# Inducing-point attention and a gated layer on one core: the last four 512-token outputs evacuated in two halves, and a new written-out order

## The chip, the cores and the metric

The kernel runs on one core of a Trainium2 chip. The metric is the device time of one execution in microseconds (us); three runs of the kernel before gave 278.44, 278.89 and 279.71 us. A core has five engines that each work through their own queue in order: TensorE (PE, with PEld for its weight loads), VectorE (DVE), ScalarE (ACT), GpSimd (POOL) and SyncE (SP), which here issues nearly all transfers. Engines wait for each other by semaphores. TensorE writes into PSUM, eight banks of 512 fp32 values in each of 128 partitions; ACT and DVE read PSUM, POOL does not.

## The reference, cut to what matters

Input `x` is 4 batches of 12800 tokens with 128 channels. `inducing` has 32 rows.

```python
def mab(q, kv):
    s = scale * (q @ kv.transpose(0, 2, 1))
    s = s - s.max(-1, keepdims=True)
    a = np.exp(s)
    a /= a.sum(-1, keepdims=True) + 1e-09
    return a @ kv
h = mab(I, x)                      # 32 rows per batch, over 12800 tokens
x = mab(x, h)                      # 12800 rows per batch, over 32 rows
...
for k in range(K):                 # K = 5, causal
    gate_pre += conv_w[k][None, None, :] * xp[:, k:k + S, :]
gate = 1.0 / (1.0 + np.exp(-gate_pre))
val = x @ w_val
return (gate * val @ w_out)
```

## The kernel before, in words

Each batch's tokens are cut into four strips of 3200, which sit side by side in the 128 partitions as four groups of 32. A strip is cut into seven chunks of mostly 416 to 512 tokens (`SIZES`). For each batch the work is:

- `load_xt`, `load_xk` (SP): the tokens with channels in the partitions (`xt`), and with tokens in the partitions (`xk`). In batch 0 `xk` is made on chip: `make_xk` transposes on PE (L315) and copies out of PSUM on ACT (L112) or DVE (L114).
- `s1` (PE L335, evacuated by DVE L351 with a running maximum), `gmax` (DVE L363, then L387 and four L373 on POOL or DVE), `e1` (exponential on ACT L395, 32x32 transposes on DVE L400), `h` (PE L419, summed by DVE L436 to L440): the first attention. `h` of the last chunks needs the maxima of all chunks.
- `prep`, `prep2`, `prep3`, `prep_out`: the 32 rows `hT` are normalised (PE L454, DVE L460 to L462), folded into the weights of the second part (POOL L487, L488, L493; PE L527; copies L112/L114), and scales are made (`osc`: four L555 and L556 on POOL or DVE).
- `s2` (PE L590, DVE L601), `joint` (DVE maximum L613, POOL L619, ACT L625, DVE sum L631 to L636, POOL L642, DVE L647, then ACT L653 and POOL L661 write the attention weights as two fp16 parts into the long strips `P1`, `P2`): the second attention's weights.
- `visit` (PE L676 for the gate's five taps, L685 for the values; ACT L747 tanh; DVE L756 gate times value), `halves` (ACT L768 and POOL L773 split the product into two fp16 parts `gh`, `gl`; `gl` has two buffers), `outp` (PE L782; evacuation with the scale `osc` by DVE L815 or ACT L817 into a tile; store by SP L822). One output is one chunk of one strip, up to 512 tokens by 128 channels, in one PSUM bank.

Nothing is scheduled at build time. Every piece of work is an entry of `Plan.ops`; `launch` emits the entries in the order of the table `TURN`, and each engine's queue has its share of them in that order. `MOVED` lists entries that go to their alternative engine (an evacuation from ACT to DVE, the small `f1` of `gmax` and `prep_out` from POOL to DVE), `BANK` gives each PSUM tile its bank, `FULL` lists outputs that PE makes with 128-column weights instead of four groups of 32. The tables were found by a search outside the kernel. Semaphore waits follow from the tiles that an instruction reads and writes.

The last two chunks of the last batch are the end of the program: chunk 5 has 512 tokens, and its four outputs use the large tiles `ss` and `et` in place of `os`; chunk 6 has 160, and its outputs come two strips at a time and skip the fp16 split.

Of the kernel before, what the change touches and what calls it, by code (L numbers as in the profile page):

```python
# [15 lines left out]
ALU = mybir.AluOpType  # L16
# [10 lines left out]
SP = 1024.0  # L27
# [57 lines left out]
def tile_kernel(ctx: ExitStack, tc: tile.TileContext, xt, xk, indT_in, w64, out):  # L85
# [13 lines left out]
    st = {}  # L99
# [27 lines left out]
    def two(key):  # L127

        return st[key].rearrange("p (a b) -> p a b", a=2)
# [658 lines left out]
    def outp(k, rs):  # L788
# [19 lines left out]

        def ev(j=len(plan.ops)):
            o = sb(pw, os, [P, OSW if os[0] == "os" else 1024])[:, :m * n]  # L810
            a = st[key][:, :n]
            if m == 2:
                o, a = o.rearrange("p (a b) -> p a b", a=2), two(key)[:, :, :n]
            if on(j) is V:
                V.tensor_scalar(o, a, st["osc", b], None, ALU.mult)  # L815
            else:
                S.activation(o, a, AF.Copy, scale=st["osc", b])  # L817

        j = op("ACT", ev, [i], [os], [key, ("osc", b)], size=m * n, alt="DVE")
# [5 lines left out]
        op("SP", store, [j], [], [os], size=m * n * 512)  # L825
# [175 lines left out]
```

## Time and profile before

| | |
|---|---|
| median of 3 runs | 278.89 us (278.44 to 279.71) |
| profiled execution | 278.53 us, of which the span of the trace is 276.4 us |
| PE busy | 263.7 us (95% of the span) |
| DVE busy | 227.6 us (82%) |
| ACT busy | 196.2 us (71%) |
| POOL busy | 194.4 us (70%) |
| moved by DMA | 73.48 MB, 266 GB/s over the span |
| PE's granted clock | 1.00 in nearly every stretch: its level of 2.4 GHz |

The busy times overlap. PE's busy time is the largest; the rest of the span is PE's waits, its start and what follows its last matmul. The stages are plain in the trace: batch 0 is loaded and summed until 32 us, its weights are made until 45 us, then the visits run with the next batch's attention beside them until about 230 us, and the last visits and outputs run alone. After the last matmul there is one evacuation, one store and its landing.

### The profile page before, as it was taken

The page shows a single profiled execution, that of the slowest core. Times are in us where ns is not written, and L with a number is a line of the kernel's source. Part 1 is how long each engine was busy: PE and PEld are TensorE (multiplying, and loading weights), DVE is VectorE, ACT ScalarE, POOL GpSimd, SP SyncE. Part 2 cuts the span into 40 slices and gives each one's busy share as a digit, 9 for nine tenths or more (in the row PEclk, how much of TensorE's full clock was granted, in tenths as well). Part 3 has the DMA queues.
Part 4 walks back from the last instruction along what each step waited for, and adds up shares of the span by engine and source line. Part 5 has one row for each costly group of instructions (what it writes and reads, how often), then busy time and mean ns, then how long its engine had stood idle before and what let it go on. Part 6 is the DMA issues. An engine that isn't in the chain of part 4 may idle for free.

```text
span 276.4 us, 10872 instructions
## 1 busy us (share of the span) xinstructions
PE 263.7 (95%) x4655; PEld 142.3 (51%) x4655; DVE 227.6 (82%) x441; ACT 196.2 (71%) x257; POOL 194.4 (70%) x152
## 2 busy tenths in 40 slices
PE   8989987999999999999999999999999999999993
PEld 4567634766434473475454356656353445443551
DVE  0688899989999977979999799869979997785680
ACT  2547248696588897875877877858878697887764
POOL 1011068976768895985799739876998898997691
PEclk9999999999999999999999999999999999999999
DMA  7999699799989889659989997633134143344467
GB/s 223 408 408 385 224 409 407 262 364 407 348 275 384 314 284 411 263 198 359 365 272 398 329 384 231 256 129 143 58 114 161 64 169 121 115 162 168 154 231 274
DMA packets 30255, 73.48 MB, mean 266 GB/s; under 512 B 3456, under 2 KB 12800, under 8 KB 30208
## 3 DMA queue, kind: packets, MB, share of 16 engines
q1 hardware_dynamic: 30064, 72.79, 71.9%
q8 instruction: 36, 0.59, 0.9%
q14 instruction: 11, 0.09, 0.1%
q10 hardware_dynamic: 144, 0.02, 0.0%
HBM read 46.57 MB, written 26.21 MB: 263 GB/s over the span
## 4 chain that ended last, share of the span: by engine, by line
PE 57%; DVE 16%; DMA 12%; ACT 4%; issue 4%; POOL 3%; SPq 1%; DVEq 0%; ACTq 0%; POOLq 0%
PE banks L676 20%; PE banks L782 17%; PE banks L419 6%; PE banks L590 5%; DMA xt<-in_xt_dram 4%; PE banks L685 4%; DVE tg L756 4%; PE banks L335 3%; DMA raw<-in_w_dram 3%; DMA xk<-in_xk_dram 2%; DMA out_dram<-os 2%; PE banks L315 2%; DVE e L601 2%; ACT os L817 2%; DVE os L815 2%
## 5 line engine op out<-in xcount | busy, mean ns | idle before, releaser
L773 POOL TENSOR_TENSOR gl<-tg,gh 128x1024 f16<-128x1024 f32 (+4 forms) x54 | 106.2, 1972 | 26.3 <-PE banks L782 12.5
L676 PE MATMUL banks<-P,W 32*128 32x512 f16 (+5 forms) x1680 | 105.5, 352 | 1.3 <-ACT W L112 1.0
L676 PEld LDWEIGHTS <-W 32*128 32x128 f16 x1680 | 54.3, 92 | 38.2 <-issue 8.6
L747 ACT ACTIVATE tg<-banks,gsc 128x1024 f32<-128x1024 f32 (+5 forms) x56 | 55.3, 1018 | 22.6 <-PE banks L676 21.4
L756 DVE SCALAR_TENSOR_TENSOR tg<-tg,banks 128x1024 f32<-128x1024 f32 (+5 forms) x56 | 60.5, 1096 | 5.7 <-PE banks L685 4.9
L782 PE MATMUL banks<-gh,wo 128*32 128x448 f16 (+6 forms) x642 | 61.6, 359 | 0.8 <-DVE tg L756 0.6
L768 ACT CAST gh<-tg 128x1024 f16<-128x1024 f32 (+4 forms) x54 | 52.0, 969 | 10.3 <-DVE tg L756 9.3
L782 PEld LDWEIGHTS <-wo 128*32 128x32 f16 (+1 forms) x963 | 31.8, 97 | 38.5 <-issue 14.8
L685 PE MATMUL banks<-P,W 32*128 32x512 f16 (+5 forms) x336 | 41.7, 353 | 2.3 <-ACT tg L747 1.5
L815 DVE TENSOR_SCALAR os<-banks,osc 128x448 f32<-128x448 f32 (+4 forms) x49 | 32.4, 688 | 11.0 <-PE banks L782 9.5
L782 PE MATMUL banks<-gl,wo 128*32 128x448 f16 (+7 forms) x321 | 40.2, 358 | 0.0
L817 ACT ACTIVATE os<-banks,osc 128x512 f32<-128x512 f32 (+4 forms) x57 | 34.9, 646 | 7.5 <-PE banks L782 6.1
L642 POOL TENSOR_TENSOR e<-e,z 128x1024 f32<-128x1024 f32 (+7 forms) x17 | 25.0, 1468 | 7.1 <-ACT tg L747 2.2
L661 POOL TENSOR_TENSOR P<-pt,P 128x1024 f16<-128x1024 f32 (+7 forms) x17 | 27.9, 1640 | 1.8 <-ACT P L653 1.7
L619 POOL TENSOR_TENSOR e<-e,m 128x1024 f32<-128x1024 f32 (+7 forms) x17 | 24.9, 1470 | 5.4 <-DVE m L613 4.8
L419 PE MATMUL banks<-xk,et 128*32 128x129 f32 x800 | 26.0, 274 | 0.3 <-DVE et L400 0.3
L419 PEld LDWEIGHTS banks<-xk,et 128*32 128x32 f32 x800 | 23.1, 110 | 5.9 <-issue 3.0
L335 PE MATMUL banks<-xt,indT 128*32 128x512 f32 (+5 forms) x224 | 25.1, 557 | 0.0
L590 PE MATMUL banks<-xt,hT 128*32 128x512 f32 (+5 forms) x224 | 24.4, 553 | 0.6 <-ACT tg L747 0.5
L351 DVE TENSOR_SCALAR_CACHE_REDUCE ss<-banks 128x1024 f32<-128x1024 f32 (+8 forms) x17 | 15.9, 933 | 8.6 <-PE banks L335 8.4
L685 PEld LDWEIGHTS <-W 32*128 32x128 f16 x336 | 14.2, 92 | 14.1 <-issue 11.6
L395 ACT ACTIVATE ss<-ss,ng 128x1024 f32<-128x1024 f32 (+8 forms) x17 | 15.5, 922 | 7.0 <-DVE ng L373 6.7
(98 smaller groups left out, 254.4 us busy)
## 6 DMA issues: line engine op xcount, KB each, us to landing
xt<-in_xt_dram SPq DMA_DIRECT2D x28, 512.0 KB, 8.1
xk<-in_xk_dram SPq DMA_DIRECT2D x25, 451.5 KB, 6.8
xt<-in_xt_dram SPq DMA_DIRECT2D x23, 448.0 KB, 7.6
out_dram<-os SPq DMA_DIRECT2D x36, 256.0 KB, 2.9
out_dram<-os SPq DMA_DIRECT2D x40, 224.0 KB, 2.6
xk<-in_xk_dram SPq DMA_DIRECT2D x15, 516.0 KB, 7.0
out_dram<-os SPq DMA_DIRECT2D x20, 240.0 KB, 2.7
out_dram<-os SPq DMA_DIRECT2D x4, 208.0 KB, 4.9
```

What stands on the lines that cost most here:

```text
L335: T.matmul(s[32 * r:32 * r + 32, at:at + n], c_["indT"], st[xkey][:, o:o + n // 32, r, :], start=True, stop=True)
L419: T.matmul(t[32 * s:32 * s + 32, :P + 1], st[et][:, at + 32 * i:at + 32 * i + 32], st[xs[c][0]][:, xs[c][1] + i, :], start=j < R, stop=j > ...
L590: T.matmul(s[32 * r:32 * r + 32, at:at + n], st["hT", b], st[xkey][:, m:m + n // 32, r, :], start=True, stop=True)
L676: T.matmul(two(("ps", "g", b, c, r // 2))[:, r % 2, :n], st["W", b][q, w, k, :], st[("P1", "P2")[e]][q, o:o + n], start=u == 0, stop=u == ...
L685: T.matmul(two(("ps", "v", b, c, r // 2))[:, r % 2, :n], st["W", b][q, w, TAPS, :], st[("P1", "P2")[e]][q, o:o + n], start=u == 0, stop=u ...
L747: S.activation(t[:, :, :n], two(("ps", "g", b, c, p))[:, :, :n], AF.Tanh, scale=st["gsc", b])
L756: V.scalar_tensor_tensor(t, t, 1.0, two(("ps", "v", b, c, p))[:, :, :n], ALU.add, ALU.mult)
L768: S.copy(sb(pw, g1, [P, 2, 512], F16)[:, :, :n], st[tg][:, :, :n])
L773: on(j).tensor_tensor(sb(pw, g2, [P, 2, 512], F16)[:, :, :n], st[tg][:, :, :n], st[g1][:, :, :n], ALU.subtract)
L782: T.matmul(t[q], w[:, q], x, start=j == 0, stop=j == len(terms) - 1)
L815: V.tensor_scalar(o, a, st["osc", b], None, ALU.mult)
L817: S.activation(o, a, AF.Copy, scale=st["osc", b])
```

## The change

`outp` gains a second evacuation for the four outputs of the last full chunk (those in `ss` and `et`): ACT takes columns 0 to 255, DVE columns 256 to 511, and the store waits for both. With the four new entries all entry numbers from there on shift, and the tables are new throughout.

```diff
+        cut = n // 2 if os[0] != "os" and m == 1 else m * n
+
         def ev(j=len(plan.ops)):
             o = sb(pw, os, [P, OSW if os[0] == "os" else 1024])[:, :m * n]
             a = st[key][:, :n]
             if m == 2:
                 o, a = o.rearrange("p (a b) -> p a b", a=2), two(key)[:, :, :n]
+            else:
+                o, a = o[:, :cut], a[:, :cut]
...
-        j = op("ACT", ev, [i], [os], [key, ("osc", b)], size=m * n, alt="DVE")
+        def ev2():
+            V.tensor_scalar(st[os][:, cut:n], st[key][:, cut:n], st["osc", b], None, ALU.mult)
+
+        js = [op("ACT", ev, [i], [os], [key, ("osc", b)], size=cut, alt="DVE" if cut == m * n else None)]
+        if cut < m * n:
+            js.append(op("DVE", ev2, [i], [], [os, key, ("osc", b)], size=n - cut))
...
-        op("SP", store, [j], [], [os], size=m * n * 512)
+        op("SP", store, js, [], [os], size=m * n * 512)
...
 TURN = [
-    0, 1, 3, 17, 18, 19, 20, 21, 22, 25, 23, 24, 4, 27, 26, 2, 28, 33, 38, 29, 31, 63, 34, 65, 64, 66, 73, 35, 32,
+    0, 1, 19, 21, 17, 18, 20, 22, 25, 4, 23, 24, 27, 26, 3, 28, 33, 38, 48, 2, 34, 39, 29, 63, 31, 40, 35, 64, 32,
```

What the tables move is seen on the engines' queues. In the changed kernel the evacuations stand at L819 (DVE), L821 (ACT) and L824 (DVE, second halves), the store at L831; lines above 800 are shifted, lower ones are not.

The start of SP's queue: the pieces of batch 0's `xt` and the weights `raw`. Before:

```order
L263 DMA xt<-in_xt_dram 128x640
L263 DMA xt<-in_xt_dram 128x384
L263 DMA xt<-in_xt_dram 128x896
L263 DMA xt<-in_xt_dram 128x768
L263 DMA xt<-in_xt_dram 128x1024 x6
L187 DMA raw<-in_w_dram 128x261
```

Changed:

```order
L263 DMA xt<-in_xt_dram 128x896
L263 DMA xt<-in_xt_dram 128x1024
L263 DMA xt<-in_xt_dram 128x640
L263 DMA xt<-in_xt_dram 128x384
L263 DMA xt<-in_xt_dram 128x768
L263 DMA xt<-in_xt_dram 128x1024 x3
L187 DMA raw<-in_w_dram 128x261
```

The first pieces of chunks 1 and 2 come ahead of chunk 0, and `raw` moves ahead of two pieces of 512 KB, those of chunk 3. The four pieces behind it are the same.

DVE's queue where batch 0's weights are made, from the maximum of the second `s2` piece (L613, 13 columns) on. Before:

```order
L613 TENSOR_REDUCE m_535<-e 128x13
L631 TENSOR_REDUCE z<-e 128x8
L633 TENSOR_SCALAR z<-z 128x24
L634 RECIPROCAL z<-z 128x8
L636 MEMSET z 32x1
L351 TENSOR_SCALAR ss,mx<-banks 128x960
L647 STREAM_TRANSPOSE pt<-e 128x256
L631 TENSOR_REDUCE z<-e 128x13
```

Changed:

```order
L613 TENSOR_REDUCE m_546<-e 128x13
L351 TENSOR_SCALAR ss,mx<-banks 128x448
L508 TENSOR_SCALAR w_548<-banks,vs 128x32
L509 SCALAR_TENSOR_TENSOR w_548<-banks,vs,w_548 128x32
L631 TENSOR_REDUCE z<-e 128x8
L633 TENSOR_SCALAR z<-z 128x24
L634 RECIPROCAL z<-z 128x8
L636 MEMSET z 32x1
L631 TENSOR_REDUCE z<-e 128x13
L633 TENSOR_SCALAR z<-z 128x39
L634 RECIPROCAL z<-z 128x13
L647 STREAM_TRANSPOSE pt<-e 128x256
```

The next batch's evacuation of 448 columns (L351) moved from ahead of the first L601 to behind the second maximum, and the sum of the second piece now stands ahead of the first piece's L647; the evacuation of 960 columns moved behind it.

The end of DVE's queue, with the semaphores that each instruction waits for. Changed:

```order
L819 TENSOR_SCALAR os<-banks,osc 128x320 [waits DMAHW5_49,PE_49]
L824 TENSOR_SCALAR et<-banks,osc 128x256 [waits Activation_49]
L824 TENSOR_SCALAR ss<-banks,osc 128x256 [waits Activation_49]
L819 TENSOR_SCALAR os<-banks,osc 128x320 [waits DMAHW6_49,DVE_49,PE_49]
L824 TENSOR_SCALAR et<-banks,osc 128x256 [waits Activation_49]
L824 TENSOR_SCALAR ss<-banks,osc 128x256 [waits Activation_49]
```

The four new second halves each wait for one semaphore, ACT's, and the four first halves on ACT (L821) for PE's. Before, the four outputs were whole evacuations on ACT:

```order
L817 ACTIVATE et<-banks,osc 128x512 [waits DVE_49,PE_49]
L817 ACTIVATE ss<-banks,osc 128x512 [waits PE_49]
L817 ACTIVATE et<-banks,osc 128x512 [waits PE_49]
L817 ACTIVATE ss<-banks,osc 128x512 [waits DVE_49,PE_49]
```

## Rows read from the trace of the kernel before

**Rows 1.** The page: busy us of each engine, share of the span, instructions.
```profile
PE 263.7 (95%) x4655; PEld 142.3 (51%) x4655; DVE 227.6 (82%) x441; ACT 196.2 (71%) x257; POOL 194.4 (70%) x152
```

**Rows 2.** Busy time by stretch: from:to, length, busy us (PE, PEld, DVE, ACT, POOL), clock, DMA share, GB/s.
```profile
0.00:10.00 10.00, 8.74 (x47) 4.61 (x48) 1.97 (x9) 2.78 (x4) 1.32 (x12) 1.00 0.82 276
10.00:20.00 10.00, 8.73 (x102) 5.70 (x101) 7.67 (x25) 4.76 (x8) 0.52 (x2) 1.00 1.03 414
...
22.10:32.22 10.12, 9.72 (x202) 7.28 (x201) 8.50 (x21) 6.13 (x8) 0.12 (x1) 1.00 0.73 265
32.22:40.72 8.50, 7.40 (x136) 2.76 (x137) 8.00 (x33) 3.10 (x6) 3.96 (x8) 1.00 1.02 409
...
47.35:100.00 52.65, 52.40 (x1041) 29.58 (x1039) 49.19 (x97) 39.66 (x52) 41.30 (x29) 1.00 0.93 329
...
200.00:220.00 20.00, 20.00 (x344) 9.36 (x340) 17.50 (x26) 15.29 (x22) 18.68 (x12) 1.00 0.35 124
```

**Rows 3.** The timeline of the head: start, length, engine, instruction, [idle before and what ended it].
```profile
15.85 1.92 PE L335 MATMUL banks<-xt,indT 128*32 128x512 f32 x16
16.35 0.30 DVE L199 TENSOR_SCALAR bt<-raw 128x261 int32<-128x261 int32 x1 [0.67 <-DMA raw<-in_w_dram]
...
22.10 1.92 PE L335 MATMUL banks<-xt,indT 128*32 128x512 f32 x16
...
32.22 0.33 PE L454 MATMUL banks<-pick,H 128*32 128x32 f32 x16 [0.40 <-DVE H L440]
```

**Rows 4.** The timeline where batch 0's weights are made.
```profile
34.01 0.60 DVE L351 TENSOR_SCALAR_CACHE_REDUCE ss<-banks 128x448 f32<-128x448 f32 x1
...
38.02 1.15 DVE L351 TENSOR_SCALAR_CACHE_REDUCE ss<-banks 128x960 f32<-128x960 f32 x1
...
39.46 0.55 DVE L631 TENSOR_REDUCE z<-e 128x13 f32<-128x416 f32 x1
...
41.59 0.61 DVE L647 STREAM_TRANSPOSE pt<-e 128x416 f32<-128x416 f32 x1
...
43.47 0.97 POOL L661 TENSOR_TENSOR P<-pt,P 128x416 f16<-128x416 f32 x1
...
44.49 0.35 PE L676 MATMUL banks<-P,W 32*128 32x416 f16 x2 [0.24 <-POOL P L661]
```

**Rows 5.** The timeline at two waits of PE for a PSUM bank.
```profile
144.89 0.99 ACT L747 ACTIVATE tg<-banks,gsc 128x896 f32<-128x896 f32 x1
...
145.94 1.33 PE L590 MATMUL banks<-xt,hT 128*32 128x448 f32 x12 [0.46 <-ACT tg L747]
...
227.34 0.87 DVE L601 STREAM_TRANSPOSE e<-banks 128x672 f32<-128x672 f32 x1
...
228.27 0.38 PE L685 MATMUL banks<-P,W 32*128 32x480 f16 x2 [0.42 <-DVE e L601]
```

**Rows 6.** The timeline of the last output.
```profile
271.50 0.40 PE L782 MATMUL banks<-gl,wo 128*32 128x512 f16 x4
...
271.94 0.69 ACT L817 ACTIVATE ss<-banks,osc 128x512 f32<-128x512 f32 x1
...
272.65 0.33 SPq L822 DMA_DIRECT2D out_dram<-ss  x1
```

**Rows 7.** Evacuations by shape: count, busy us, mean ns of one, idle before.
```profile
L817 ACT ACTIVATE os<-banks,osc 128x512 f32<-128x512 f32 x21 | 13.9, 686 | 2.6 <-PE banks L782 2.5
...
L815 DVE TENSOR_SCALAR os<-banks,osc 128x512 f32<-128x512 f32 x15 | 11.0, 745 | 5.1 <-PE banks L782 5.1
...
L815 DVE TENSOR_SCALAR os<-banks,osc 128x416 f32<-128x416 f32 x4 | 2.3, 633 | 0.0
...
L817 ACT ACTIVATE os<-banks,osc 128x224 f32<-128x224 f32 x4 | 1.5, 447 | 1.0 <-PE banks L782 1.0
```

**Rows 8.** The small `f1` instructions: ns of one, minimum, median and maximum, by engine.
```profile
L555 DVE TENSOR_SCALAR u<-qm x12: 201/204/207, 98.3 to 221.8; 32x1 f32<-32x1 f32 x12
L555 POOL TENSOR_SCALAR u<-qm x4: 278/282/286, 45.9 to 47.0; 32x1 f32<-32x1 f32 x4
```

More of the change, by code (lines that the diff above doesn't have):

```diff
@@ L883 @@
 TURN = [
[51 rows of a table removed]
[52 rows of a table added]
 ]
 MOVED = [
[4 rows of a table removed]
[4 rows of a table added]
 ]
 BANK = [
[9 rows of a table removed]
[9 rows of a table added]
 ]
 FULL = [
-    832, 835, 838, 850, 856, 859, 994, 997, 1000, 1003, 1006, 1009, 1012, 1015, 1030, 1033, 1036, 1039, 1042, 1045,
-    1048, 1051, 1054, 1057, 1060, 1063, 1066, 1069, 1072, 1075, 1078, 1081, 1084, 1087, 1093, 1096, 1099,
+    850, 856, 859, 985, 988, 991, 994, 997, 1000, 1003, 1018, 1021, 1024, 1027, 1042, 1045, 1048, 1051, 1054, 1057,
+    1060, 1063, 1066, 1069, 1072, 1075, 1078, 1081, 1084, 1087, 1090, 1093, 1096, 1099, 1102, 1106, 1110, 1114,
+    1118, 1121,
 ]
```

127 rows, old and new, of tables (BANK, MOVED, TURN) are left out of this document.

## The prediction

> **What bounds the kernel now.** I read the page's busy times first, then the windows by stage, then the timelines at the start, where batch 0's weights are made, at PE's waits, and at the end. The busy times [rows 1] say that PE is the engine to watch: 263.7 of 276.4 us. The clock column of the windows stands at 1.00 throughout, the 2.4 GHz level [rows 2], so no term below is a clock. The windows say where PE is not the limit. From 47.35 to 100 us it is busy 52.40 of 52.65 us, but from 32.22 to 40.72 us only 7.40 of 8.50, with DVE at 8.00 [rows 2]. So there are three places where time can be had: the head up to 32.22 us, set by transfers and by a chain through DVE; the making of batch 0's weights after it; and the end, where one evacuation and one store follow PE's last matmul. In between only waits of PE for a PSUM bank or for a late operand count, and they are short: the two that I looked up are 0.46 and 0.42 us [rows 5].
>
> PE's work itself does not change. Both kernels have the same visits, sums and outputs; three more outputs use 128-column weights, which stream the same columns, and I cost that at nothing.
>
> **The halves.** This is the part that the title names, and the order decides it. Each second half on DVE waits for ACT, not for PE: the four L824 rows each name ACT's semaphore. Since the first half is the last thing ACT has done by then, DVE starts when ACT ends, so the halves run one after the other. The last output now: PE's last matmuls begin at 271.50 and run 0.40, ACT starts at 271.94, takes 0.69, and the store issues at 272.65 [rows 6]. An ACT evacuation takes 447 ns at 224 columns and 686 at 512, so 256 take about 447 + 32 x 239/288 = 474 ns. DVE takes 633 at 416 and 745 at 512; along that line 256 take about 633 - 160 x 112/96 = 446 ns, but the lone fixed cost may be more, so I take 0.48 [rows 7]. From ACT to PE a hand-over is 145.88 to 145.94, and from DVE to PE 228.21 to 228.27: 0.06 us [rows 5]. The sum is 0.47 + 0.06 + 0.48 = 1.01 us in place of 0.69: **+0.3 us** at the very end, where nothing covers it. Bounds: 0.2 us for the hand-over makes it +0.5; halves that did overlap would give 0.48 - 0.69 = -0.2. The first three of the four outputs cost nothing: ACT kept up with PE at 0.69 us for a whole one, and either half is shorter. SP's four stores wait for DVE now instead of ACT, with nothing behind them but each other.
>
> The Trainium skill, "PSUM — Partial Sum Buffer", section "PSUM bank collisions raise a hardware error", says that two engines may not be in the same bank and 32-partition group at once, reads against reads included, and that the compiler's scheduler adds a dependency between them. One 512-token output is one bank, so by that rule the two halves cannot run at once, which speaks against the change; the wait in the order has that shape, and no run yet shows its length.
>
> **The head.** `raw` (0.27 MB) now goes ahead of chunk 3's pieces (1.05 MB). Counting bytes down SP's queue (128 partitions by the columns of its rows, 4 bytes each, 8 for `raw`), `raw` ended at 4.79 MB before. The first 10 us move 2.76 MB and the next run at 0.414 MB/us [rows 2], so 4.79 MB have moved at 14.9 us; DVE got `raw` at 16.35 [rows 3], about 1.45 us later. The same count gives chunk 3 at 4.52 MB: 14.25 + 1.45 = 15.7, and its `s1` began at 15.85 [rows 3], so this stage runs as its data arrive. Now chunk 3 ends at 4.79 MB and its `s1` begins about 0.5 us later. The last piece of batch 0 ends at 6.89 MB in both orders: 20.0 + 1.45 = 21.45 us. The `s1` on it began at 22.10 before [rows 3], behind three groups of transposes. In the new order PE has the same three groups before it, but reaches them sooner, since `h` of chunks 0 and 1 and chunk 4's transposes are done back to back rather than in the gaps. So it can begin at 21.5: -0.6 us, and no earlier. From there both orders have the same list on PE: one `h`, three groups of eight transposes, four `h`; it took 10.12 us with 9.72 busy [rows 2], the last 0.40 a wait for DVE's sum [rows 3]. DVE's chain behind that `s1` is the same, with one weights instruction less in it; I take 0.3 of the 0.40. The head: **-0.9 us**, with 0 and -1.2 as ends. That the first transposes start on a larger first piece (448 KB for 320) costs some tenths there, hidden because the stage is paced by the arrivals behind it.
>
> **Batch 0's weights.** Before, DVE emptied a 448-column bank of the next batch (34.01, 0.60 us) ahead of the first L601, and a 960-column one (38.02, 1.15) ahead of the first L647; the second sum came after (39.46, 0.55, and its reciprocals), the second L647 at 41.59, and PE began the second chunk's gate at 44.49 after POOL's L661 [rows 4]. From the head's end that is 44.49 - 32.22 = 12.27 us. Now the 448 columns come after the second maximum and the sums stand together. The first piece gets later: the second piece's sum (0.55 and two short instructions) stands in its way instead of the 1.15, which is a little less, and the 0.60 has moved from the front of its chain into the middle, together with the `s2` weights' two rows; I take about +0.4. The second piece, which releases the gate that PE waits longest for, gains what it no longer waits behind, about **-0.4 us**. Ends: +0.5 (the first piece decides) and -1.0.
>
> **The two bank waits.** At 145.94 PE waits 0.46 us for ACT's second tanh to free bank 4; in the new order that `s2` uses bank 0, which was emptied long before. At 228.27 it waits 0.42 us for DVE's L601 [rows 5]; now three outputs instead of two lie between that `s2` and the visit that follows. Both gone: -0.9. But the new banks bring short turn-rounds of their own, visits that start one output after the bank's last use; I set +0.5 against it: **-0.4 us**, ends -0.9 and +0.9.
>
> **The sum.** +0.3 - 0.9 - 0.4 - 0.4 = -1.4 us against the profiled execution's 278.53, so **277.1 us**. That execution is 0.36 under the median of 278.89 and near the fastest run, 278.44; I do not shift the sum.
>
> **The rivals.** *The lead is eaten.* The head's 1.3 us reach 47 us, and then DVE takes them: it is busy 49.19 of 52.65 us up to 100 us [rows 2]. For it: DVE feeds every visit there. Against it: PE is busy 52.40 of the same window, and DVE's list gets shorter. Then only the end's +0.3 and some bank waits are left: 278.5 to 279.1 us, no change.
>
> *POOL becomes the bound* (slower). The new `MOVED` leaves five small `f1` groups, net, on POOL that DVE did before: the scales `osc` of batches 1 to 3 and two of `gmax`. An `f1` of `osc` is four instructions of 0.282 us on POOL against 0.204 on DVE [rows 8], with two more of the kind: at least 1.7 us of POOL's queue each, and behind it stand `gl` products that PE's outputs wait for. From 200 to 220 us POOL is busy 18.68 of 20 us [rows 2], so its 1.3 us of slack are less than one such group. It decides if two of the groups fall where POOL has no slack: 2 x 1.7 - 1.4 + 278.5 gives 280.5 us, and all five 8.5 - 1.4 + 278.5 = 285.6. Against it: the order puts another POOL instruction, batch 3's second L642, later in that stage.
>
> *The halves do run at once.* Then the end gives -0.2 in place of +0.3: 276.6 us. The order's waits speak against it.
>
> *A better middle.* Of PE's waits after 47 us that are not a change between strips of 32 rows and whole columns, I know of two; if the new order removes as many again without new ones, -1 us more: about 275.5.
>
> **How the numbers follow.** The forecast with its small sides (276.5 to 277.5) has 0.27, a better middle 0.14, halves at once 0.03, the lead eaten or replaced by new waits 0.34, POOL or another queue as the bound 0.22. About 0.5%, 1.4 us, is what a measurement of this kernel can tell from no change: faster is below 277.5, slower above 280.3. That makes faster 0.44, same 0.34, slower 0.22. The range reaches from 275.0, a better middle with the head's lower end, to 280.6, two groups on a full POOL; about 1 in 10 lies beyond either end.
>
> **What would show it.** Each L824 begins within 0.1 us of the end of its L821, and the last store issues about 1.0 us after PE's last matmul instead of 0.75. Chunk 3's `s1` begins near 16.4 us and the last `s1` of batch 0 near 21.5; PE's L454 comes near 31.3 us and the second chunk's gate near 43.2. PE waits for no bank before the third `s2` of batch 2. The forecast is wrong if L454 comes as late as 32 us, if POOL's rows show no idle time around `osc`, or if PE's first matmul of the last visits comes no earlier than before.

## The result and the profile after

The changed kernel takes **275.45 us** (median of 5 runs, 274.88 to 275.82) against 278.89 (278.44 to 279.71): a ratio of 0.987 with an interval of 0.985 to 0.989. The direction and the range were right, the size was not: 277.1 had been forecast. The profiled execution took 275.18 us with a span of 273.4, against 278.53 and 276.4: 3.35 us less, where the sum said 1.4. About a third of the executions (57 of 156) of the kernel before and of those that keep its order at 42 to 46 us, but 1 of 58 with the new order there, show a mean granted clock of 0.986 to 0.994 and take 1 to 3 us longer; they are in the medians and the ratios, which makes the experiments' ratios of the new order up to 0.2% too low.

The busy line of the page after, which answers to [rows 1]:

```profile
PE 261.3 (96%) x4622; PEld 141.0 (52%) x4622; DVE 226.6 (83%) x420; ACT 194.6 (71%) x254; POOL 201.7 (74%) x180
```

PE is still the bound. Its work is the same, yet it is busy 2.4 us less: a group of matmuls counts as busy while single matmuls in it wait. POOL has 7.3 us more.

The timeline of the head and of batch 0's weights, for [rows 3, 4] (start, length, engine, instruction, idle before):

```profile
13.53 0.29 DVE L199 TENSOR_SCALAR bt<-raw 128x261 int32<-128x261 int32 x1
...
15.98 0.63 PE L335 MATMUL banks<-xt,indT 128*32 128x512 f32 x3
...
21.57 1.92 PE L335 MATMUL banks<-xt,indT 128*32 128x512 f32 x16 [0.73 <-DVE et L400]
...
31.47 0.33 PE L454 MATMUL banks<-pick,H 128*32 128x32 f32 x16 [0.57 <-DVE H L440]
...
43.25 0.35 PE L676 MATMUL banks<-P,W 32*128 32x416 f16 x2 [0.15 <-POOL P L661]
```

`raw` is first read 2.8 us sooner, the last `s1` of batch 0 begins at 21.57 (22.10 before), L454 at 31.47 (32.22), and the second chunk's gate at 43.25 (44.49). So PE is 0.75 us ahead after the head and 1.24 after the weights.

From there to the first output of batch 3's chunk 3, the windows of before and then of after (length, busy us of PE, PEld, DVE, ACT, POOL, clock, DMA share, GB/s), each with PE's row at which the window ends:

```profile
44.49:259.37 214.88, 212.91 (x3893) 112.05 (x3892) 187.66 (x333) 164.44 (x213) 175.13 (x114) 1.00 0.70 251
...
259.37 0.60 PE L782 MATMUL banks<-gh,wo 128*128 128x512 f16 x2
```

```profile
43.25:255.05 211.80, 211.02 (x3928) 109.71 (x3927) 184.64 (x308) 164.34 (x211) 182.65 (x142) 1.00 0.72 259
...
255.05 0.60 PE L782 MATMUL banks<-gh,wo 128*128 128x512 f16 x2
```

The same PE work took **3.08 us less** (214.88 - 211.80), and the lead grew to 4.32. Only 1.19 of the 3.08 is idle time between groups (1.97 against 0.78); the rest stood inside "busy". The waits view of PE from 47 us to the end, before and then after (what waited <- for what: us, times, longest), shows both that the middle got clean and that something new came:

```profile
PE banks L782 <- DVE tg L756: 0.6, 3, 0.2
PE banks L590 <- ACT tg L747: 0.5, 1, 0.5
PE banks L685 <- DVE e L601: 0.4, 1, 0.4
PE banks L685 <- DVE os L815: 0.3, 1, 0.3
```

```profile
PE banks L782 <- DVE tg L756: 1.7, 1, 1.7
PE banks L676 <- DVE os L819: 0.3, 2, 0.2
PE banks L782 <- ACT tg L747: 0.3, 1, 0.3
PE banks L419 <- DVE et L400: 0.3, 1, 0.3
```

The two waits of [rows 5] (before: L590 for ACT, L685 for L601) are gone. The 1.7 is one stall in the tail. The timeline there, after:

```profile
261.72 4.11 SPq L831 DMA_DIRECT2D out_dram<-os  x4
...
263.75 0.75 DVE L819 TENSOR_SCALAR os<-banks,osc 128x512 f32<-128x512 f32 x1 [2.06 <-PE banks L782]
264.42 0.87 DVE L756 SCALAR_TENSOR_TENSOR tg<-tg,banks 128x320 f32<-128x320 f32 x2
...
265.35 0.81 PE L782 MATMUL banks<-tg,wof 128*128 128x160 f32 x4 [1.71 <-DVE tg L756]
```

PE waits for a product of chunk 6 on DVE (L756), and that product stands behind an evacuation of chunk 4 (L819) on the same queue. The row puts that evacuation's wait down to PE, but PE had ended at 261.4; what came at the right moment is an earlier store out of the `os` buffer that it writes, whose last part landed at 263.63 by the trace's completion records. The chain of waits goes through such a store:

```profile
259.59 4.74 DMA out_dram<-os
```

The last output, for [rows 6]:

```profile
268.48 0.59 PE L782 MATMUL banks<-gh,wo 128*128 128x512 f16 x2
...
268.92 0.38 PE L782 MATMUL banks<-gl,wo 128*128 128x512 f16 x1
...
269.33 0.47 ACT L821 ACTIVATE ss<-banks,osc 128x256 f32<-128x256 f32 x1 [0.17 <-PE banks L782]
...
269.84 0.48 DVE L824 TENSOR_SCALAR ss<-banks,osc 128x256 f32<-128x256 f32 x1 [0.16 <-ACT ss L821]
...
270.35 0.33 SPq L831 DMA_DIRECT2D out_dram<-ss  x1
```

ACT 0.47, DVE 0.48, one behind the other, as in the prediction's sum. The store issues 1.05 us after PE's last matmul ends at 269.30; before it was 0.75. From that issue to the end of the span it is 3.05 us (3.75 before).

The account, in us of the span:

| Part | Forecast | Measured |
|---|---|---|
| head, to L454 | -0.9 | -0.75 |
| batch 0's weights, L454 to the second chunk's gate | -0.4 | -0.49 |
| middle, that gate to batch 3's chunk 3 | -0.4 | -3.08 |
| tail, to the last output's first matmul (271.07, now 268.48) | 0 | +1.73 |
| halves, to the last store's issue | +0.3 | +0.3 |
| last store, issue to end | 0 | -0.70 |

They sum to -3.0 of the span; 0.3 more lie outside it (2.1 to 1.8). These are single executions. The middle, taken between the same two matmuls at about 45 and 258 us, lasts 212.7 to 212.8 us in the kernel before and in two experiments with its order (the halves, the sixth buffer), and 209.7 to 211.2 in the ten profiled kernels with the new order: a gain of 1.6 to 3.1, median 2.8. So the direction of that row is sure, and -3.08 is its upper end.

### The profile page after: what moved, and what is told of

The parts are those of the page before. It is cut to its first block, busy times and chain, and to the rows that moved or that the text cites. A ratio compares the mean times of both kernels' runs of the same rounds, so it can differ in the third digit from the quotient of the medians.

```text
span 273.4 us, 10792 instructions
## 1 busy us (share of the span) xinstructions
PE 261.3 (96%) x4622; PEld 141.0 (52%) x4622; DVE 226.6 (83%) x420; ACT 194.6 (71%) x254; POOL 201.7 (74%) x180
## 4 chain that ended last, share of the span: by engine, by line
PE 76%; DVE 12%; POOL 3%; issue 2%; ACT 2%; DMA 2%; SPq 0%; DVEq 0%
PE banks L676 26%; PE banks L782 20%; PE banks L419 7%; PE banks L685 6%; PE banks L335 6%; PE banks L590 6%; PE banks L315 3%; DMA out_dram<-os 2%; DVE tg L756 2%; DVE os L819 1%; PE banks L840 1%; DVE z L631 1%; DVE ss L351 1%; DVE et L400 1%; DVE e L601 1%
## 5 line engine op out<-in xcount | busy, mean ns | idle before, releaser
L676 PEld LDWEIGHTS <-W 32*128 32x128 f16 x1680 | 52.6, 92 | 39.0 <-issue 7.4
L756 DVE SCALAR_TENSOR_TENSOR tg<-tg,banks 128x1024 f32<-128x1024 f32 (+5 forms) x56 | 60.2, 1094 | 4.7 <-PE banks L685 2.2
L782 PE MATMUL banks<-gh,wo 128*32 128x448 f16 (+7 forms) x636 | 61.6, 358 | 0.3 <-ACT tg L747 0.3
L819 DVE TENSOR_SCALAR os<-banks,osc 128x512 f32<-128x512 f32 (+4 forms) x52 | 34.7, 693 | 12.8 <-PE banks L782 12.1
L685 PE MATMUL banks<-P,W 32*128 32x512 f16 (+5 forms) x336 | 41.6, 353 | 0.8 <-ACT tg L747 0.7
L821 ACT ACTIVATE os<-banks,osc 128x448 f32<-128x448 f32 (+4 forms) x54 | 33.4, 643 | 9.6 <-PE banks L782 6.4
L419 PE MATMUL banks<-xk,et 128*32 128x129 f32 x800 | 25.4, 274 | 0.3 <-DVE et L400 0.3
L590 PE MATMUL banks<-xt,hT 128*32 128x512 f32 (+5 forms) x224 | 24.7, 552 | 0.0
L351 DVE TENSOR_SCALAR_CACHE_REDUCE ss<-banks 128x1024 f32<-128x1024 f32 (+8 forms) x17 | 15.9, 933 | 9.4 <-PE banks L335 9.4
L685 PEld LDWEIGHTS <-W 32*128 32x128 f16 x336 | 13.9, 92 | 12.4 <-issue 9.9
L625 ACT ACTIVATE e<-e 128x1024 f32<-128x1024 f32 (+7 forms) x17 | 14.3, 841 | 7.2 <-POOL e L619 7.2
```

Of the source, the lines that this page charges most:

```text
L419: T.matmul(t[32 * s:32 * s + 32, :P + 1], st[et][:, at + 32 * i:at + 32 * i + 32], st[xs[c][0]][:, xs[c][1] + i, :], start=j < R, stop=j > ...
L590: T.matmul(s[32 * r:32 * r + 32, at:at + n], st["hT", b], st[xkey][:, m:m + n // 32, r, :], start=True, stop=True)
L676: T.matmul(two(("ps", "g", b, c, r // 2))[:, r % 2, :n], st["W", b][q, w, k, :], st[("P1", "P2")[e]][q, o:o + n], start=u == 0, stop=u == ...
L685: T.matmul(two(("ps", "v", b, c, r // 2))[:, r % 2, :n], st["W", b][q, w, TAPS, :], st[("P1", "P2")[e]][q, o:o + n], start=u == 0, stop=u ...
L756: V.scalar_tensor_tensor(t, t, 1.0, two(("ps", "v", b, c, p))[:, :, :n], ALU.add, ALU.mult)
L782: T.matmul(t[q], w[:, q], x, start=j == 0, stop=j == len(terms) - 1)
```

## The experiments

None of these kernels leaves out work. Numbers on times are medians of the runs with a ratio to the kernel before on the same chip and its interval.

**Undoing one part each.** The new order with the four outputs evacuated whole by ACT, and the old order with the halves (each second half right behind its first):

```diff
-        js = [op("ACT", ev, [i], [os], [key, ("osc", b)], size=cut, ...)]
-        if cut < m * n:
-            js.append(op("DVE", ev2, [i], [], [os, key, ("osc", b)], size=n - cut))
+        j = op("ACT", ev, [i], [os], [key, ("osc", b)], size=m * n, alt="DVE")
```

> The changed kernel's order, with the last four outputs evacuated whole by ScalarE as before. Theory 1 (the halves run one after the other and their 0.3 us lies on the path to the last store; the gain is wholly the new order's): about 0.3 us faster than the changed kernel, 275.2 us, 3.7 under the kernel before. Rival (the halves give part of the gain): slower than the changed kernel by 0.2 us or more, 275.7 us.

275.39 us, ratio 0.985 [0.981, 0.989]: from 275.45 the runs can't tell it. In the timelines the last output's first matmul to the store's issue is 268.91 to 270.47, 1.56 us, against 1.87 in the changed kernel, and to the end of the span 4.59 against 4.92. The halves cost 0.3 there. This profiled run wins nothing by it, because its PE reaches the last output 0.43 us later than the changed kernel's; the medians can't show 0.3.

> The kernel before with nothing new but the halves: each second half stands directly behind its first. Theory 1 (the 0.3 us lie on the path): 0.3 us slower than before. Theory 2 (the end of the kernel before is set by its last four stores, which land 0.7 us apart whatever comes ahead of them): 0.0 us. Rival (halves at once): 0.2 us faster.

279.2 us, 1.000 [0.997, 1.003]. The issue is later by the same 0.3, 271.15 to 273.04, 1.89 against 1.58, as the timeline shows:

```profile
272.02 0.47 ACT L821 ACTIVATE ss<-banks,osc 128x256 f32<-128x256 f32 x1 [0.17 <-PE banks L782]
...
272.53 0.48 DVE L824 TENSOR_SCALAR ss<-banks,osc 128x256 f32<-128x256 f32 x1 [0.16 <-ACT ss L821]
...
273.04 0.33 SPq L831 DMA_DIRECT2D out_dram<-ss  x1
```

But to the end of the span it is 5.35 against 5.33: nothing. The last store, issued 0.3 later, lands 2.65 us after its issue instead of 2.94. In the old order the last stores had a backlog ahead of them anyhow. A window of the kernel before:

```profile
272.00:274.00 2.00, 0.00 (x0) 0.00 (x0) 0.00 (x0) 0.63 (x1) 0.00 (x0) 1.00 1.04 381
```

Only ACT's last evacuation still runs, and the DMA engines are full at 381 GB/s: 0.69 us for each 256 KB store. So the title's part gains nothing in either order (in the new one it costs 0.3 by the timelines, below what the times can tell); the gain is the order's.

**Which part of the order.** The entries of all four tables are taken from one kernel up to a place and from the other behind it; first the place is in the first visits (some 45 us), then ahead of L454 (some 32 us). As a scheme:

```diff
-TURN = NEW
+TURN = NEW[:n] + [e for e in OLD if e not in NEW[:n]]
```

> The changed order up to the second chunk's gate (about 45 us), the order of the kernel before from there on, whole evacuations. Parts that add up: 1.25 us faster than before (277.6 us), the lead that the changed kernel has at that gate. Rival 1 (DVE eats the lead in the visits that follow): 0.0 us. Rival 2 (a lead at the start is what removes PE's short waits later): about 3 us faster.

281.98 us, 1.009 [1.005, 1.012]: slower, by its seam, the place where the two orders meet. The waits of PE, 44 to 50 us:

```profile
PE banks L335 <- ACT tg L747: 3.1, 1, 3.1
```

An `s1` of the old order got a bank that the new head still holds. It is a failed experiment on the head and a good one on what a delay does: PE stands 2.11 us behind the kernel before at 53 us and 2.21 behind at 272. A shift passed through 220 us of this program nearly whole.

> The order of the kernel before up to the second chunk's gate, the changed order and the halves from there on. Parts that add up: the changed kernel's gain of 3.4 us less the head's 1.25, so 2.2 us faster than before (276.7 us). Rival 1 (the head's lead is eaten, so the rest carries all): 3.4 us faster. Rival 2 (the lead removes the later waits): little or nothing, 0 to 0.4 us.

278.2 us, 0.997 [0.994, 0.999]; its seam costs some 2 us too, and it stays 3.10 us behind the changed kernel at 55 us and 3.05 at 265.

> The changed order up to the last sum of batch 0's first attention (PE's L454 at 31 to 32 us), where both orders have done the same work, and the order of the kernel before from there on, whole evacuations. If a lead passes one to one from there to the end: 0.7 to 0.9 us faster than before, 278.2 us. Rival 1 (the lead is eaten): 0.0 us. Rival 2 (the later order fits only its own head, as in the run with the cut at 45 us): slower than before by over 1 us.

278.62 us, 0.997 [0.995, 1.000]: 0.8 us less by the ratio, with 0.1 to 1.4 as its interval. The head alone is worth what the timeline gives it, 0.75, as far as the runs can tell.

> The other way round: the order of the kernel before up to PE's L454, the changed order and the halves from there on. Parts that add up: 3.4 less 0.8, so 2.6 us faster than before, 276.4 us. Rival 1 (the rest carries all): 3.4 us faster. Rival 2 (it fits only its own head): 0 to 1 us faster.

276.11 us, 0.988 [0.985, 0.992]: everything but the head gives 3.3 us (2.4 to 4.3). It is 1.25 us behind the changed kernel at L454 and 1.44 at 260 us. The two parts make 4.1 together where the whole gives 3.6 (3.0 to 4.2): within the intervals they add up, and the late stretch stays late, so nothing eats the lead. How well one execution repeats another limits this: in the profiled one with the new head alone PE was 0.95 us behind the kernel before at 105 us and 1.88 at 215, though the order there is that of before.

**What made the middle faster.** Three rivals to "many short waits went away": a sixth output buffer, which the changed kernel does not have but whose lack could be what the old order suffers from; the bank that the prediction named at the wait of 228.27; and the small groups on POOL.

```diff
-        c_["zero"] = const.tile([P, 512], F16, name="zero")
+        c_["zero"] = st["P1"][:, :512]
...
-BUFS = dict(... os=5, ...)
+BUFS = dict(... os=6, ...)
```

> The kernel before with six os buffers for five (room is made by keeping the warm-up's zeros in P1). Theory B (late landings of stores keep evacuations, and what stands behind them, waiting all through the kernel, and this is the largest part of what the new order saves after 47 us): 1 to 2 us faster, and PE gains between 50 and 250 us. Rival (the short waits after 47 us come from banks and from the order on DVE, ACT and POOL; buffers matter only in the last 15 us): PE's course up to 250 us is that of before within 0.3 us, and the end gains 0 to 0.9 us.

279.03 us, 1.000 [0.998, 1.003], and PE's course within 0.2 us of before all the way: buffers aren't it. The bank exchange, as a scheme:

```diff
-BANK of ("ps", "v", 3, 0, 0): 2, of ("ps", "g", 3, 1, 0): 4
+BANK of ("ps", "v", 3, 0, 0): 4, of ("ps", "g", 3, 1, 0): 2
```

> The kernel before with two banks exchanged: the first values of batch 3 in banks 4 and 5, the gates of its second chunk in 2 and 3, so that PE's wait of 0.42 us at 228.27 us has no cause. If a wait that goes is a gain of its own size at the end: 0.4 us faster. Rivals: it comes back as a wait at that gate (0.0 us), or it is worth more because later waits go with it (over 0.8 us).

280.39 us, 1.004 [1.001, 1.007]. The waits of PE from 225 to 245 us, in which the kernel before has one of 0.4 for L601:

```profile
PE banks L782 <- ACT tg L747: 0.6, 1, 0.6
PE banks L685 <- ACT os L817: 0.4, 1, 0.4
```

The wait at 228.27 [rows 5] went, and a longer and another one came behind it. To take one bank out of a full rotation moved the wait on; it didn't remove it.

```diff
 MOVED = [
-    30, 37, 45, 74, 80, 90, 119, 207, 234, 236, 304, 310, 339, 407, 413, 442, 803, ...
+    30, 37, 45, 74, 80, 90, 119, 234, 310, 407, 413, 803, ...
```

> The kernel before with only the five small f1 groups moved from VectorE to GpSimd that the changed tables leave there (osc of batches 1 to 3, gmax of batch 1's last and batch 2's first chunks). If GpSimd becomes the bound: 1.7 us slower for one group on a full queue, 5 us or more for all. If it has room: within 0.3 us of before. If VectorE's relief is what frees PE after 47 us: 1 us or more faster.

283.48 us, 1.016 [1.013, 1.019]: five `f1` groups on POOL in the old order cost 4.4 us. PE's waits from 55 to 100 us (before: one of 0.2), and below them one of POOL's:

```profile
PE banks L419 <- DVE tg L756: 1.3, 1, 1.3
PE banks L676 <- ACT tg L747: 0.7, 1, 0.7
PE banks L685 <- ACT os L817: 0.6, 1, 0.6
PE banks L590 <- ACT tg L747: 0.6, 1, 0.6
```

```profile
POOL e L619 <- DVE m L613: 3.4, 2, 2.0
```

So the slower rival's price is real in the old order: 4.4 us in all, about 0.9 a group where the prediction had 1.7. Its mechanism, a POOL without slack, does not show. In that stretch POOL is busy 34.24 of 45 us (34.33 before), its wait for DVE was 3.0 us before already, and PE waits for DVE and ACT, not for POOL. By what way the five groups make DVE and ACT late stays open. In the changed kernel, whose `f1` are all 16 on POOL at 281 ns, the same groups cost nothing that shows.

**What made the stall in the tail.** If the evacuation's buffer is what is late, chunk 4's outputs of batch 3 in free `xk` tiles take the stall away:

```diff
-        os = (... if k == len(seqs) - 2 else "os", "out", b, c, rs[0])
+        os = (... if k == len(seqs) - 2 else "xk" if k == len(seqs) - 3 else "os", "out", b, c, rs[0])
...
-            o = sb(pw, os, ...)[:, :m * n]
+            o = sb(pxk if os[0] == "xk" else pw, os, ...)[:, :m * n]
```

> The changed kernel with the four outputs of chunk 4 of the last batch written into tiles of the pool that held xk (free by then) in place of os. Theory B (VectorE's evacuation at 263.75 us stands waiting for an os buffer whose store lands late, and the gate product that PE needs stands behind it): PE's wait of 1.71 us before the first output of chunk 6 falls under 0.4 us, the last stores come 1.0 to 1.8 us earlier, 273.7 to 274.5 us. Rival (the product was waiting for its own inputs, tanh or values): the wait stays, 275.4 us.

273.67 us, 0.979 [0.976, 0.981]: 1.8 us under the changed kernel by the medians. Its tail:

```profile
262.49 1.40 DVE L819 TENSOR_SCALAR xk<-banks,osc 128x512 f32<-128x512 f32 x2
...
263.81 0.88 DVE L756 SCALAR_TENSOR_TENSOR tg<-tg,banks 128x320 f32<-128x320 f32 x2
...
265.01 0.71 PE L782 MATMUL banks<-tg,wof 128*128 128x160 f32 x4
```

Both evacuations run back to back, L756 follows, and PE's row has no wait. The other way to free L756 is to put it ahead of the evacuation (two banks are exchanged as well, so that it may):

```diff
-    ... 783, 1094, 1091, 1100, 789, 788, ...
+    ... 783, 1094, 1091, 789, 788, 1100, ...
```

> The changed kernel with the two gate products of chunk 6 ahead of the last evacuation of chunk 4 in VectorE's queue (and two PSUM banks of chunk 5's outputs exchanged). Buffers as they are. Theory B: PE's 1.71 us wait goes, but the evacuation still starts at 263.7 and the three stores behind it still issue from 264.5 on, so that the transfers at the end give back only 0.7 to 0.8 us: 274.7 us. Rival 1 (PE alone sets the end): 1.7 us, 273.7 us. Rival 2 (the product waits for its own inputs): 275.4 us.

274.96 us, 0.983 [0.980, 0.985]. PE's wait is gone here too, but the evacuation (264.35, [0.39 <-DMA]) is later, the stores behind it go out from 265.13 on, and from the last output's first matmul to the end it is 5.88 us instead of 4.92. PE, 0.91 us behind the changed kernel at 257 us, ends 1.06 ahead of it, and the stores gave back 0.96 of these 1.97 us. PE's end alone isn't the kernel's end.

Why is that store late? Around it the chip fetched instructions: the page has 36 packets of 16 KB on queue 8, and the DMA view from 259.5 to 261.6 us, after, has one of them:

```profile
q1 hardware_dynamic: 413, 0.75, 97.6%
q8 instruction: 1, 0.02, 4.9%
```

4.9% of 16 engines in 2.1 us is 1.65 us, the length of this one packet (1.64 from 259.70). Of the 16 parts of the store out of the buffer in question 15 had landed by 261.69 and the last at 263.63. Other stores show the same: from 160 us on, 30 of the changed kernel's 67 stores were under way during a fetch, and 14 of these have a last part that lands over 0.6 us behind the one before it (up to 2.0); of the other 37 it is two, each in the wake of a fetch. To move the fetch, chunk 2's four outputs of batch 3 go in strips (72 more records on PE, loads and matmuls):

```diff
-    1060, 1063, 1066, 1069, 1072, 1075, 1078,
+    1060, 1063, 1078,
```

> The changed kernel with the four outputs of chunk 2 of the last batch made in strips of 32 rows in place of 128-column weights: the same sums and columns, but 9 more matmuls and weight loads each, some 72 more records of PE. Theory F (the stores from 258.7 us on land 2 us late on one of 16 engines because a 16 KB fetch of PE's instructions occupies it at 259.7): that fetch comes about 2 us earlier, between two groups of stores, and PE's 1.71 us wait shrinks to under 0.7: 1.0 to 1.7 us faster than the changed kernel, 274.0 us. Rival (the landing is late for another reason, or for the number of stores): the wait stays, 275.4 us or a little more.

274.54 us, 0.984 [0.981, 0.988]. The packet came 0.9 us sooner (258.82 for 259.70) and took 0.93 us instead of 1.64, and the last part of the store landed 0.9 us behind the others instead of 1.9. The timeline there:

```profile
262.81 0.75 DVE L819 TENSOR_SCALAR os<-banks,osc 128x512 f32<-128x512 f32 x1 [1.20 <-PE banks L782]
...
264.41 0.40 PE L782 MATMUL banks<-tg,wof 128*128 128x160 f32 x1 [0.86 <-DVE tg L756]
```

The evacuation began at 262.81 for 263.75, and PE's loss fell from 1.88 to 1.03 us. That fits a fetch as the cause, but the packet moved by less than its own length, and other stores lay around it as before, so the fetch is made likely, not proved; how it holds up one part of a store isn't seen.

**Better versions.** Each has the spare tiles: with whole evacuations and with the halves in two banks, and both of these with the product moved first as well. The halves in two banks:

```diff
+                if cut < m * n:
+                    for h, s in ((0, slice(0, cut)), (512, slice(cut, n))):
+                        columns(t[:, h:h + n // 2], [... st[g1][:, q, s] ...], parts(i))
+                    continue
...
-            V.tensor_scalar(st[os][:, cut:n], st[key][:, cut:n], ...)
+            V.tensor_scalar(st[os][:, cut:n], st[key][:, 512:512 + n - cut], ...)
```

> The changed order with chunk 4's outputs in the spare tiles, the two gate products of chunk 6 first, and the last four outputs evacuated whole by ScalarE: the best of the parts. Theory 1: the spare tiles' 1.8 us and 0.3 for the halves, so 273.3 us, about 2.1 under the changed kernel. Rival (the last transfers give the 0.3 back): 273.7 us, as with the spare tiles alone.

Whole, with the product first: 274.04 us, 0.982 [0.979, 0.986]: the product ahead delays the evacuation and all stores behind it, as in the run above.

> As the run with the spare tiles, but each of the last four outputs is made in two PSUM banks, 256 tokens in each, so that ScalarE and VectorE read different banks. Theory 1 (the halves wait for each other because they share a bank): VectorE's half no longer waits for ScalarE's, the last store issues 0.5 us or a little more after PE's last matmul ends instead of 1.05, and the time is 0.4 to 0.6 us under the run with the spare tiles, 273.1 us. Rival (the two engines still take turns): 1.0 us to the issue, 273.7 us.

Two banks, with the product first: 274.49 us, 0.984 [0.980, 0.987]. The moved product makes this no clean test of its halves.

> The changed order with the spare tiles and whole evacuations, without the product moved ahead. Theory 1: 0.3 us under the run with the spare tiles and the halves, 273.4 us, since the last four stores each issue 0.3 us earlier and none waits in SP's queue. Rival (the transfers at the end take it back, as in the run that also moved the product): 273.7 us or more.

Whole: 273.58 us, 0.979 [0.976, 0.982].

> The changed order with the spare tiles and the last four outputs in two banks each, without the product moved ahead. Theory 1: each of VectorE's halves begins before ScalarE's ends, the last store issues 0.5 to 0.6 us after PE's last matmul ends, and the time is 0.4 to 0.5 under the run with the spare tiles: 273.2 us. Rival (the transfers at the end take it back): the store issues as early, but the time stays at 273.7 us.

Two banks: 273.36 us, 0.979 [0.976, 0.982]. Its last output:

```profile
266.92 0.47 ACT L825 ACTIVATE ss<-banks,osc 128x256 f32<-128x256 f32 x1 [0.18 <-PE banks L782]
...
267.25 0.48 DVE L828 TENSOR_SCALAR ss<-banks,osc 128x256 f32<-128x256 f32 x1 [0.17 <-PE banks L782]
267.80 0.33 SPq L835 DMA_DIRECT2D out_dram<-ss  x1
```

In two banks the halves do run at once: DVE starts 0.14 us before ACT ends and waits for PE, not for ACT. The store issues some 0.6 us after PE's last matmul, where the change has 1.05. But it ends 3.8 us later, at 271.6, exactly where the span of the whole evacuations ends. Of its last store 15 of 16 parts land 0.4 us sooner than in the whole version (270.30 for 270.70), the last part does not (270.82 for 270.76). In this execution the last store's transfer sets the end, and what is saved ahead of it is waited for behind. Both versions beat both kernels, and which is the better can't be told; the whole evacuation is the simpler.

## Why the prediction was right in direction and wrong in size

**The halves: right.** +0.3 us to the issue of the last store, from 0.47 + 0.04 + 0.48. Each L824 began 0.04 us after its L821, and the rule that the prediction weighed against the change, no two engines in one bank and 32-partition group at once (the Trainium skill, "PSUM — Partial Sum Buffer", section "PSUM bank collisions raise a hardware error"), agrees with what ran: in one bank one behind the other, in two banks at once. It isn't a test of the rule, since in one bank the kernel's own semaphore orders the halves, and no run leaves it out. What the sum lacked is that nothing follows from the issue alone: the stores' own backlog hid the 0.3 in the old order.

**The head and the weights: right.** -0.75 for -0.9, -0.49 for -0.4. The last `s1` began at 21.57 (forecast 21.5), 0.13 us after its last piece had landed at 21.44 (21.45), and the gate at 43.25 (43.2). Two details were off. Chunk 3's `s1` did not wait for its data until 16.4: they had landed at 15.34, 1 us before the count by bytes, and it began at 15.98, behind the sums ahead of it. And the wait for DVE's sum ahead of L454 did not fall by 0.3 but rose from 0.40 to 0.57.

**The middle: the step that failed.** "The two bank waits" was priced at -0.4 and measured -3.08. The mechanism, fewer waits for late banks and operands, is borne out as far as the rows go: both waits went, and PE shows no wait for a bank from 47 us to the third `s2` of batch 2, as forecast. The count was wrong. The prediction looked up two waits of PE and called the rest short. They can be counted instead: cut PE's row into pieces (up to 36 matmuls of visits, or one run of any other line), take each from its start to the next one's, and subtract its columns' time at the pace that rows without a wait come near (0.213 us for 512 fp16 columns, where such rows show 0.216; twice that in fp32). That time is 198.1 us in both traces, so the middle holds 16.7 us of excess before and 13.7 after. Before, ten pieces stretch by more than 0.35 us, 4.5 us in all, and only two of them are the known ones (0.64 and 0.61); after it is four, 1.7 us. Pieces with 0.2 to 0.35 us of excess went from 3.5 to 2.9 us, and all smaller ones stayed (8.7 and 9.0). So 2.8 of the 3.1 us are long stretches, of which the prediction knew two. Of the four after, two are new (0.52 and 0.41), where +0.5 had been set against the 0.9 of the known waits; the others stood before at much the same length. Most of the excess never shows as idle time of PE, which is why a look at idle rows and at the waits view missed it.

That each stretch is a wait is argued from its length, not seen in a row. And what in the order removed them, sequence, banks or engines, isn't separated and stays open: the single bank exchange and the groups moved to POOL, each alone in the old order, made it slower, and a sixth buffer did nothing.

**The tail: the term that is missing.** The sum has no term between the middle and the last output, and there +1.73 us was lost to an evacuation that waited for its buffer with the last gate's product behind it. The rows at the end of DVE's queue, which stand with the change, show two later evacuations (L819) that wait for a DMA's semaphore in this way; the prediction read those rows for the halves only. The last store, from issue to landing, has no term either: it gave 0.70 back, as the old order issued it into a backlog.

**What was luck.** By its own words the rival "a better middle", 1 us more than the forecast, gives 276.1 and not its 275.5, and by the same count the range begins at 275.8, above the 275.45 that was measured. That 275.5 came so near is luck: the middle was 2.7 us better than the sum had it, and the tail and the last store took back 1.0 of that.

**The rivals.** "The lead is eaten" fell: shifts made in the head or ahead of the middle are still there at its end. "POOL becomes the bound" did not happen here. In the old order the move of five groups costs 4.4 us, but not by a full POOL. "The halves do run at once" needs two banks, and then gained nothing that the times show. "A better middle" had the mechanism, with a chance of 0.14.

## What to carry to other kernels

Where one engine is busy from end to end, count what each of its pieces takes against the same piece without a wait, over the whole stage, before pricing a new order by the waits that are easy to find: idle time between groups was less than half of what was to be had. A lead won early stayed to the end here wherever that engine's order was kept, so price it at full value; but an evacuation that waits for its output buffer holds up whatever stands behind it on its engine, and a look at the last few instructions of each queue with their waits would have shown it. At the very end look first at what the stores still have to move: splitting the last evacuation was worth nothing here while they set the end.

## What the runs showed of the hardware

An instruction fetch of 16 KB took 1.64 us at 259.70 (0.93 in the run that moved it), and stores that were under way during one often landed late with one of their 16 parts (14 of 30, against 2 of 37). A store has landed with its last part: 4.74 us for the store of the chain, where the median of the 36 such stores is 3.2. That the fetch takes the DMA engine of the late part is not seen in any row.

In the profile of the new head with the old order from L454 on (280.40 us) the granted clock fell. The windows:

```profile
42.00:44.00 2.00, 0.60 (x14) 0.35 (x17) 2.00 (x3) 2.00 (x5) 1.83 (x4) 1.00 1.02 410
44.00:46.00 2.00, 2.00 (x34) 1.76 (x28) 1.04 (x2) 1.72 (x4) 1.66 (x5) 0.52 1.03 412
```

After PE was busy 0.60 of 2.00 us, waiting for batch 0's weights, it was granted 0.52 in the next two, so nearly all of them at 1.2 of the two levels, 1.2 and 2.4 GHz. PE, 0.73 us ahead of the kernel before until then, was 0.95 behind it afterwards. The changed kernel's PE is busy 1.22 us from 42 to 44 and its clock stayed at 1.00; before's is busy 0.46 there, and its profiled clock stayed at 1.00 too, so a short stretch of rest doesn't decide it by itself.
